# Attention row maxima put back by query: through PE's transposition or through DRAM

## The chip, the core and the metric

One core of a Trainium2 chip runs one program. The metric is the device time of one execution in microseconds (us). The engines that matter here are TensorE (PE, whose weight loads are listed as PEld), VectorE (DVE), ScalarE (ACT), GpSimd (POOL) and the queue of SyncE (SP, listed as SPq), which issues nearly all DMA transfers. All of them work through their own instructions in order and wait for each other by semaphores.

## The reference

A pre-norm transformer block on 2048 tokens of width 640: 32 heads of width 20, then a gated feed-forward part of width 1728.

```python
h = x + attention(layernorm(x))          # softmax(q k^T / sqrt(20)) v, then @ wo
h2 = h + (silu(n @ w_gate) * (n @ w_up)) @ w_down      # n = layernorm(h)
```

Everything is float32. The softmax is computed with its row maximum subtracted.

## The kernel before

Three stages follow each other. The first (to about 337 us) normalizes the tokens and projects queries, keys and values. The second is the attention (about 337 to 1545 us). The third is the feed-forward part.

The attention is worked in 32 *units*: 8 groups of four heads, each with 4 chunks of 512 queries. Unit `u` is group `u // 4`, chunk `u % 4`. Each unit has 16 *slots*, one for every 128 keys (`kt`). `now[0]` counts the slots, so unit `u` begins with slot `16 * u`. In a slot PE does four score products (`scores`, L890, the letters s and S of `ORDER`), each followed by an exponential on ACT (L896), and eight small products of weights and values of the slot two before (`weigh`, L900, the letter W).

The row maximum is not subtracted by an engine. Scores are products over 62 rows: 60 hold queries and keys split into a rounded and a rest part, and the rows 60 and 61 of the queries' tile `q_stk` hold the negated maximum of every query, as a rounded part and a rest; the same rows of the keys' tile hold ones. So a unit's scores can start only when these rows are filled, and the maximum must be known before. It is computed ahead by a product of its own over 60 rows (`max_one`, L181, the letters m and M) and a maximum over keys on DVE (L187). These run ahead of the scores: a unit's last maximum comes 5 to 14 slots before its first score.

With the last of them, `max_all` reduces over the key blocks on DVE (L194, tile `neg`: 128 queries on the partitions, 16 numbers each), and POOL splits the result into the rounded part and the rest (L198 and L199, tile `both`, 128 x 32). Queries stand on the partitions there, and must lie along a row in `q_stk`. `max_finish` does that: PE transposes `both` (L206) to a 32 x 128 tile in PSUM, which takes one of the four buffers `ps_one` that the scores use too; ACT copies it to SBUF (L208, tile `m2`, in the profile `m`); four DMA transfers on SP's queue (L213) bring 8 rows of 128 numbers each to the four places, a row 512 B in one piece. It is called two slots after the last maximum:

```python
closing[a[0]] = now[0] + 2
```

and stands in that slot behind the letter W, ahead of the next piece of the weights' preparation (`preparing`, POOL's splitting of the feed-forward weights with loads and stores on SP's queue).

Other work on SP's queue in these slots: the next keys and values (L143, L160) and the queries of unit `u + 3`; the row sums of the unit before (`r<-o`, L913, at slot 1 of a unit), their reciprocals to DRAM and spread over partitions (`r_d`, `rb`, L923 and L929, after slot 4), the divided output (L938, after slot 11). POOL multiplies by `rb` at slot 9 (L935). Every transfer on the queue signals one of eight semaphores in turn, and waits for the transfer that used it before; an instruction that waits holds up those behind it.

Of the kernel before, what the change touches and what calls it, by code (L numbers as in the profile page):

```python
# [9 lines left out]
F32 = mybir.dt.float32  # L10
BF16 = mybir.dt.bfloat16
F32R = mybir.dt.float32r
I32 = mybir.dt.int32
AF = mybir.ActivationFunctionType
# [3 lines left out]
P = 128  # L18
S = 2048
D = 640  # L20
H = 32
# [5 lines left out]
NC = S // CH  # L27
TPC = CH // P
NF = (F + P - 1) // P
G = 4  # L30
NG = H // G
# [12 lines left out]
def tile_block(ctx: ExitStack, tc: tile.TileContext, x, wqkv, wo, wg, wu, wd, out):  # L44
    nc = tc.nc
# [4 lines left out]
    dram = ctx.enter_context(tc.tile_pool(name="dram", bufs=1, space=bass.MemoryType.DRAM))  # L50
    qk_d = dram.tile([2, NG, 2, GD, S], F32R, name="qk_d")
    v_d = dram.tile([S, NG, VG], F32, name="v_d")
    o_d = dram.tile([D, S], F32, name="o_d")
    r_d = dram.tile([H, S], F32, name="r_d")
    z_d = [dram.tile([P, 2 * ND * CH], F32R, name=f"z_d{c}") for c in range(2)]
    t_d = [dram.tile([P, 8 * CH], F32R, name=f"t_d{i}") for i in range(2)]
# [14 lines left out]
    def ps_one():  # L71
        return psum.tile([P, CH], F32, name="ps_one", tag="ps_one", bufs=2)

    ident = const.tile([P, P], F32, name="ident")
# [50 lines left out]
    stk = att_ctx.enter_context(tc.tile_pool(name="stk", bufs=1, side="right"))  # L125
    k_stk = [stay.tile([P, 2, S], F32R, name="k_stk0", tag="first")]
    v_stk = [stay.tile([P, NT, VG], F32, name="v_stk0", tag="second")]
    keys, queries, values = {}, {}, {}
# [5 lines left out]
    ends = {}  # L134
# [42 lines left out]
    def max_one(u, kc, t, pair, b):  # L177

        ps = ps_max()
        rows = slice(b * ROW, b * ROW + NPART)  # L180
        nc.tensor.matmul(  # L181
            ps,
            queries[u][rows, pair, t * P : (t + 1) * P],
            keys[u // NC][rows, pair, kc * CH : (kc + 1) * CH],
            start=True, stop=True,
        )
        nc.vector.tensor_reduce(  # L187
            mxs[u][:, b, pair, t, kc : kc + 1], ps, axis=AX.X, op=ALU.max
        )

    def max_all(u):

        neg = stk.tile([P, G * TPC], F32, name="neg", tag="neg", bufs=2)
        nc.vector.tensor_reduce(  # L194
            neg, mxs[u].rearrange("p b h t k -> p (b h t) k"), axis=AX.X, op=ALU.max, negate=True
        )
        ends[u] = stk.tile([P, 2, G * TPC], F32R, name="both", tag="both", bufs=2)
        nc.gpsimd.tensor_copy(ends[u][:, 0], neg)  # L198
        nc.gpsimd.tensor_tensor(  # L199
            out=ends[u][:, 1], in0=neg, in1=ends[u][:, 0].bitcast(F32), op=ALU.subtract  # L200
        )

    def max_finish(u):

        m = ps_one()[: 2 * G * TPC, :P]
        nc.tensor.transpose(m, ends.pop(u).bitcast(F32).rearrange("p i n -> p (i n)"), ident)  # L206
        m2 = stk.tile([2 * G * TPC, P], F32R, name="m2", tag="m2", bufs=1)
        nc.scalar.activation(m2, m, AF.Copy)  # L208
        for b in range(2):
            for i in range(2):  # L210
                row = b * ROW + NPART + i
                first = (2 * i + b) * 2 * TPC
                nc.sync.dma_start(  # L213
                    queries[u][row : row + 1].bitcast(F32).rearrange(
                        "r j (t p) -> r (j t) p", t=TPC
                    ),
                    m2[first : first + 2 * TPC, :].bitcast(F32),
                )

    def in_projections(u, kc, t):  # L220

# [30 lines left out]
    with tc.tile_pool(name="pa", bufs=2) as pa:  # L252
# [245 lines left out]
        first = [("block", 0, 1), ("none",)] + [("block", m) for m in range(2, 2 * ND)]  # L498
# [4 lines left out]
        for c in range(NC):  # L503
# [7 lines left out]
            for j, (kind, *which) in enumerate(work):  # L511
# [21 lines left out]
                if 0 in ends:  # L533
                    finish_at = min(finish_at, slot[0] + 2)
                    if slot[0] == finish_at:
                        max_finish(0)
# [405 lines left out]
    todo, tail, accs, closing, now = [], [], {}, {}, [0]  # L942
# [3 lines left out]
    def next_max(b):  # L946
        if singles[b]:
            a = singles[b].pop(0)
            max_one(*a)
            left[a[0]] -= 1  # L950
            if left[a[0]] == 0:
                max_all(a[0])
                quiet[0] = now[0]
                closing[a[0]] = now[0] + 2

    def weigh_next():
        u, kt, probs = todo.pop(0)
# [10 lines left out]
    for u in range(NU):  # L968
        g, c = divmod(u, NC)
        if g == NG - 1 and c >= 2:  # L970
            _, first, ln, flips, _ = ahead
            extra = [*first, ln[0], lambda: None, ln[1], lambda: None, *flips]
        for kt in range(NT):
# [5 lines left out]
            for op in order:  # L979
                if op in "mM":  # L980
                    next_max(int(op == "M"))
                elif op in "sS":
                    scores(u, kt, heads[op == "S"].pop(0), probs)
                else:
                    if len(todo) == 2:
                        weigh_next()
                    for v in ready:
                        max_finish(v)
                    if extra:
                        extra.pop(0)()  # L990
                    if preparing and u and kt not in (3, 4) and quiet[0] != now[0]:
                        preparing.pop(0)()
                    if now[0] == (NU - NC) * NT + 8:
                        unit_ring, last_ring = weight_rings()
                        unit_ring.fill()
                        last_ring.fill()
# [41 lines left out]
    u, o, r = tail.pop()  # L1038
# [559 lines left out]
```

## Time and profile before

| what | value |
|---|---|
| median of 3 runs | 2111.13 us (2111.03 to 2113.79) |
| the profiled execution | 2112.34 us, of which its span is 2110.6 us |
| PE busy | 2077.2 us (98%) |
| DVE, ACT, POOL busy | 1752.9, 1295.9, 704.8 us |
| granted TensorE clock | 0.998 |
| DMA packets | 199673, 295.27 MB |

The profile has one execution. A line such as `L206 PE MATMUL ps_one<-ident,both` names the line of the kernel, the engine, the operation, the tile written and the tiles read. In the timeline the first number is the start and the second the duration; PE's rows merge instructions of one line that follow each other, and their ends overlap the next row's start, since products are pipelined: the distance from one start to the next is what an instruction costs PE.

### The profile page before, as it was taken

How to read it: one execution, taken by the hardware profiler on the slowest of the kernel's cores; microseconds unless marked ns; L12 is line 12 of the kernel's file. 1: busy time of each engine (PE TensorE's matmuls, PEld its weight loads, DVE VectorE, ACT ScalarE, POOL GpSimd, SP SyncE). 2: the span in 40 equal slices, each digit the busy share in tenths (PEclk: the TensorE clock that was granted, in tenths of full speed). 3: DMA queues.
4: the chain of work that ended last, by engine and by line, in shares of the span. 5: the costliest groups of instructions: out<-in, count | busy, mean ns of one | idle time of the engine just before them, and what ended most of it. 6: DMA issues, size and time to landing. Idle time of an engine off the chain costs nothing.

```text
span 2110.6 us, 35576 instructions
## 1 busy us (share of the span) xinstructions
PE 2077.2 (98%) x12606; PEld 1205.3 (57%) x12606; DVE 1752.9 (83%) x2901; ACT 1295.9 (61%) x2571; POOL 704.8 (33%) x1009
## 2 busy tenths in 40 slices
PE   7999999999999999999999999999999999999998
PEld 5766675333333333333333333335578888888887
DVE  6999997999999999999999999996358766666676
ACT  3222216999999999999999999996743222212221
POOL 3222212343343433353420001001135434653555
PEclk9999999999999999999999999999999999999999
DMA  7565432343433524533432113132137755884542
GB/s 253 168 190 166 153 119 82 122 122 106 150 115 102 169 89 136 165 136 126 136 110 75 33 38 88 33 100 76 35 121 262 266 171 186 300 299 158 197 152 92
DMA packets 199673, 295.27 MB, mean 140 GB/s; under 512 B 46840, under 2 KB 81656, under 8 KB 198472
## 3 DMA queue, kind: packets, MB, share of 16 engines
q1 hardware_dynamic: 185912, 266.77, 39.1%
q10 hardware_dynamic: 13584, 26.23, 4.0%
q8 instruction: 101, 1.65, 0.4%
q14 instruction: 76, 0.62, 0.1%
HBM read 196.44 MB, written 95.68 MB: 138 GB/s over the span
## 4 chain that ended last, share of the span: by engine, by line
PE 89%; DVE 5%; DMA 3%; POOL 1%; issue 1%; ACT 1%; SPq 0%; ACTq 0%; POOLq 0%; DVEq 0%
PE acc L900 24%; PE ps_max L181 15%; PE ps_one L890 15%; PE ps_a L1063 15%; PE ps_b L1157 8%; PE ps_one L422 4%; DVE mx L175 3%; PE ps_one L459 2%; PE ps_wide L171 2%; PE ps_max L628 2%; PE ps_b L628 1%; DMA qk_d<-e 1%; DMA raw<-qk_d 1%; DVE mx L187 1%; DMA halves<-j_d 1%
## 5 line engine op out<-in xcount | busy, mean ns | idle before, releaser
L896 ACT ACTIVATE probs<-ps_one 128x512 f32<-128x512 f32 x2048 | 1045.4, 623 | 131.9 <-PE ps_one L890 126.9
L187 DVE TENSOR_REDUCE mx<-ps_max 128x1 f32<-128x512 f32 x1632 | 1021.0, 683 | 95.7 <-PE ps_max L181 51.9
L890 PE MATMUL ps_one<-q_stk,k_stk 62*128 62x512 f32 x2048 | 551.1, 421 | 0.7 <-ACT e L265 0.7
L900 PE MATMUL acc<-probs,v_stk 128*32 128x512 f32 x4096 | 545.2, 604 | 0.3
L181 PE MATMUL ps_max<-k_stk,q_stk 60*128 60x512 f32 x1632 | 540.5, 459 | 2.4 <-DVE mx L187 1.5
L181 PEld LDWEIGHTS ps_max<-k_stk,q_stk 60*128 60x128 f32 x1632 | 230.2, 184 | 427.6 <-DVE mx L187 411.2
L890 PEld LDWEIGHTS ps_one<-q_stk,k_stk 62*128 62x128 f32 x2048 | 299.7, 185 | 81.6 <-ACT probs L896 52.3
L175 DVE TENSOR_REDUCE mx<-ps_wide 128x2 f32<-128x1024 f32 x208 | 240.5, 1217 | 16.2 <-PE ps_wide L171 16.0
L1278 DVE TENSOR_TENSOR tmp<-ps_a,tmp 128x512 f32<-128x512 f32 x208 | 141.2, 689 | 120.2 <-PE ps_a L1063 94.5
L1157 PE MATMUL ps_b<-halves,yp 128*128 128x320 f32 x1032 | 179.3, 308 | 1.8 <-POOL yp L81 1.2
L1157 PEld LDWEIGHTS ps_b<-halves,yp 128*128 128x128 f32 x1032 | 165.1, 188 | 18.4 <-POOL yp L81 1.5
L900 PEld LDWEIGHTS acc<-probs,v_stk 128*32 128x32 f32 x4096 | 80.6, 108 | 160.2 <-issue 152.1
L198 POOL CAST both<-neg 128x16 fp32r<-128x16 f32 x32 | 6.6, 206 | 467.6 <-DVE neg L194 212.5
L1063 PE MATMUL ps_a<-t,units 128*128 128x512 f32 x624 | 162.5, 396 | 0.0
L1063 PE MATMUL ps_a<-z,units 128*128 128x512 f32 x516 | 133.8, 394 | 0.0
L1063 PEld LDWEIGHTS ps_a<-t,units 128*128 128x128 f32 x624 | 112.6, 188 | 18.6
L81 POOL TENSOR_TENSOR yp<-y,yp 128x256 fp32r<-128x256 f32 x96 | 60.3, 628 | 187.8 <-ACT yp L80 187.8
L1162 DVE TENSOR_TENSOR h<-ps_b,h 128x320 f32<-128x320 f32 x248 | 110.1, 481 | 6.8 <-PE ps_b L1157 5.4
L1063 PEld LDWEIGHTS ps_a<-z,units 128*128 128x128 f32 x516 | 93.1, 187 | 15.9
L1063 PE MATMUL ps_a<-z,lasts 128*128 128x512 f32 x324 | 92.5, 393 | 0.0
L80 ACT ACTIVATE yp<-tmp 128x512 fp32r<-128x512 f32 x40 | 25.3, 632 | 103.2 <-POOL tmp L1150 103.2
L265 ACT ACTIVATE e<-ps_one 128x512 f32<-128x512 f32 x31 | 18.5, 598 | 107.3 <-PE ps_one L422 72.4
(164 smaller groups left out, 2066.6 us busy)
## 6 DMA issues: line engine op xcount, KB each, us to landing
units<-w_d SPq DMA_DIRECT2D x186, 256.0 KB
w_d<-stage SPq DMA_DIRECT2D x106, 256.0 KB
halves<-j_d SPq DMA_DIRECT2D x70, 320.0 KB
j_d<-stage SPq DMA_DIRECT2D x42, 320.0 KB
raw<-qk_d SPq DMA_DIRECT2D x70, 160.0 KB
k_stk<-qk_d SPq DMA_DIRECT2D x64, 160.0 KB
q_stk<-qk_d SPq DMA_DIRECT2D x64, 160.0 KB
rb<-r_d SPq DMA_DIRECT2D x32, 256.0 KB
```

The source lines that it names most:

```text
L175: nc.vector.tensor_reduce(mx[:, :, pair, t, kc], ps, axis=AX.X, op=ALU.max)
L181: nc.tensor.matmul(ps, queries[u][rows, pair, t * P : (t + 1) * P], keys[u // NC][rows, pair, kc * CH : (kc + 1) * CH], start=True, stop=True,
L187: nc.vector.tensor_reduce(mxs[u][:, b, pair, t, kc : kc + 1], ps, axis=AX.X, op=ALU.max)
L422: nc.tensor.matmul(ps, w[:, k, m * P : (m + 1) * P], a[:, k, :], start=(n == 0 and k == 0), stop=(n == 2 and k == ND - 1),)
L628: nc.tensor.matmul(ps[:, :HALF], a[:, k, :], w[:, k, hs], start=(n == 0), stop=(n == 3 * ND - 1),)
L890: nc.tensor.matmul(ps, keys[u // NC][rows, p, kt * P : (kt + 1) * P], queries[u][rows, p, :], start=True, stop=True,)
L896: nc.scalar.activation(probs[p][:, b, :], ps, AF.Exp, scale=scale)
L900: nc.tensor.matmul(acc[32 * j : 32 * j + 32, :], values[u // NC][:, kt, j * VW : j * VW + 32], probs[j // 2][:, j % 2, :], start=(kt == 0) ...
L1063: nc.tensor.matmul(ps.rearrange("p (t n) -> p t n", t=TPC), w[k][:, i], z[k][:, :, j], start=(first and m == 0), stop=(last and m == len(n ...
L1157: nc.tensor.matmul(ps, a, b, start=(n == 0), stop=(n == len(pairs) - 1))
L1162: nc.vector.tensor_tensor(out=h, in0=ps, in1=h, op=ALU.add)
L1278: add = lambda out, ps, x: nc.vector.tensor_tensor(out=out, in0=ps, in1=x, op=ALU.add)
```

## The change

`max_finish` no longer uses PE and ACT. One DMA transfer stores the tile `both` to a DRAM tile `m_d[u]`, 128 rows (queries) of 32 numbers. Four transfers load from it into the rows of `q_stk`: each takes 8 columns of all 128 rows, with the columns outermost, so numbers that follow each other in the destination lie 128 B apart in DRAM. Each load moves 1024 numbers, 4 B each, and waits for the store, since it reads what that wrote. `max_finish` is called one slot after the last maximum, not two; for unit 0, which is handled in the first stage, the place stays.

```diff
+    m_d = [dram.tile([P, 2 * H // NG * TPC], F32, name=f"m_d{u}") for u in range(NG * NC)]
...
     def max_finish(u):
 
-        m = ps_one()[: 2 * G * TPC, :P]
-        nc.tensor.transpose(m, ends.pop(u).bitcast(F32).rearrange("p i n -> p (i n)"), ident)
-        m2 = stk.tile([2 * G * TPC, P], F32R, name="m2", tag="m2", bufs=1)
-        nc.scalar.activation(m2, m, AF.Copy)
+        both = ends.pop(u).bitcast(F32)
+        nc.sync.dma_start(m_d[u], both.rearrange("p i n -> p (i n)"))
         for b in range(2):
             for i in range(2):
                 row = b * ROW + NPART + i
-                first = (2 * i + b) * 2 * TPC
-                nc.sync.dma_start(
-                    queries[u][row : row + 1].bitcast(F32).rearrange(
-                        "r j (t p) -> r (j t) p", t=TPC
-                    ),
-                    m2[first : first + 2 * TPC, :].bitcast(F32),
-                )
+                n = (i * 2 + b) * 2 * TPC
+                dst = queries[u][row : row + 1].bitcast(F32).rearrange("r j (t p) -> r (j t) p", p=P)
+                nc.sync.dma_start(dst, m_d[u][:, n : n + 2 * TPC].rearrange("p n -> n p").unsqueeze(0))
...
-                closing[a[0]] = now[0] + 2
+                closing[a[0]] = now[0] + 1
```

In the built program each of the four loads has 1024 elements of one number on its destination's side, and 8 by 128 elements of one number on its source's side. PE has 32 transpositions fewer, ACT 32 copies fewer and SP 32 transfers more.

## The prediction

> **What bounds the kernel now.** I read the page first, then the busy times of the attention by a window, then the waits in that window.
>
> ```profile
> span 2110.6 us, 35576 instructions
> PE 2077.2 (98%) x12606; PEld 1205.3 (57%) x12606; DVE 1752.9 (83%) x2901; ACT 1295.9 (61%) x2571; POOL 704.8 (33%) x1009
> DMA packets 199673, 295.27 MB, mean 140 GB/s; under 512 B 46840, under 2 KB 81656, under 8 KB 198472
> ```
>
> ```profile
> core 0: us, PE busy (x) PEld busy (x) DVE busy (x) ACT busy (x) POOL busy (x), PEclk, DMA share, GB/s
> 340.00:1480.00 1140.00, 1137.40 (x7664) 456.53 (x7663) 1036.86 (x1726) 1021.53 (x2035) 316.65 (x527) 1.00 0.34 104
> ```
>
> ```profile
> PEld ps_max L181 <- DVE mx L187: 410.2, 609, 1.1
> ACT probs L896 <- PE ps_one L890: 113.0, 303, 3.4
> POOL sums L740 <- DMA raw<-in_B_w_up: 109.9, 12, 16.7
> PEld ps_one L890 <- ACT probs L896: 44.8, 178, 0.8
> ```
>
> PE is busy in 1137.4 of 1140 us of the attention, so what PE is relieved of there comes off the time, up to the next bound. That is near: DVE has 1036.9 us and ACT 1021.5 us, so both have some 100 us of room in 1140, about ten times what follows. The large wait of PEld for DVE is the weight load standing ready early; PE itself hardly idles. The DMA engines are 34% used and POOL 28%: both have cover.
>
> **What is taken away.** Per unit one transposition, one copy on ACT and four short transfers.
>
> ```profile
> L206 PE MATMUL ps_one<-ident,both x32: 284/284/286, 314.1 to 1479.4; 128*32 128x128 f32 x32
> L208 ACT ACTIVATE m<-ps_one x32: 261/266/268, 314.4 to 1479.7; 32x128 fp32r<-32x128 f32 x32
> L213 SPq DMA_DIRECT2D q_stk<-m x128: 620/635/1357, 314.7 to 1482.1; - x128
> ```
>
> PE's duration of 0.284 us overlaps its neighbours, so I take distances of starts. Here is a slot with the transposition and the next one without it.
>
> ```profile
> 727.74 1.07 PE L900 MATMUL acc<-probs,v_stk 128*32 128x512 f32 x8
> 728.73 0.28 PE L206 MATMUL ps_one<-ident,both 128*32 128x128 f32 x1
> 728.95 0.50 PE L181 MATMUL ps_max<-k_stk,q_stk 60*128 60x512 f32 x2
> 729.86 1.06 PE L900 MATMUL acc<-probs,v_stk 128*32 128x512 f32 x8
> 730.85 0.51 PE L181 MATMUL ps_max<-k_stk,q_stk 60*128 60x512 f32 x2
> ```
>
> From the start of the eight products to the next other one are 0.99 us without it (730.85 - 729.86) and 1.21 us with it (728.95 - 727.74): it costs 0.22 us of PE. Its other cost is indirect: it takes one of four `ps_one` buffers out of the scores' turn until ACT has copied it, and the copy puts the exponentials behind it off by 0.266 us, for which PE then waits in some cases (the 44.8 us above). So one unit saves between 0.22 us (the copy is hidden) and 0.22 + 0.27 = 0.49 us (all of it comes through). I take 0.28 us, nearer to the lower end since ACT has room. Of the 32, 31 lie in the attention: 31 x 0.28 = 8.7 us (6.8 to 15). The 32nd, in the first stage, I set at nothing.
>
> **What is added: the way through DRAM.** Per unit one store, a wait for it, and four loads of 1024 numbers each, all on SP's queue. PE sees none of it unless the rows arrive after the unit's first score is due. So I need two lengths: how long the way takes from the end of `both`, and how long there is.
>
> The trace has no transfer of single numbers from DRAM. The nearest row for a store that a load waits for, and for small pieces, is that of the reciprocals: 128 pieces of 64 B to DRAM, and the load that reads them.
>
> ```profile
> 1334.99 0.60 SPq L923 DMA_DIRECT2D r_d<-r  x1
> 1336.99 0.58 SPq L929 DMA_DIRECT2D rb<-r_d  x1
> ```
>
> ```profile
> DMA packets 132, 0.01 MB, mean 26 GB/s; under 512 B 132, under 2 KB 132, under 8 KB 132
> q1 hardware_dynamic: 132, 0.01, 27.8%
> ```
>
> The load is issued 2.0 us after its store. The second fence is the window of 1336.20 to 1336.52 us, which holds that store's packets alone: 132 of them, 128 of data and 4 that signal the end, so it ran on four DMA engines, the size of its outermost dimension in DRAM (4 heads). The 27.8% of 16 engines in 0.32 us make 4.4 engines: these four were busy all along, with 33 packets each, so one packet took at most 0.32 / 33 = 9.7 ns of an engine. The loads that are to go show the same rule.
>
> ```profile
> 1480.00 2.77 SPq L213 DMA_DIRECT2D q_stk<-m  x4
> DMA  0000000000002000001000001000001000000000
> DMA packets 64, 0.02 MB, mean 4 GB/s; under 512 B 32, under 2 KB 64, under 8 KB 64
> ```
>
> Four loads leave 64 packets, 32 of data and 32 of signals: 8 engines each, as their outermost dimension is 8. The second and third row are the window 1480.0 to 1484.5 us in 40 slices of 0.11 us: the first packets fly in the 13th, 1.3 us after the issue. The new loads have 8 outermost on the source's side, so I count 8 engines with 128 numbers each.
>
> At 9.7 ns a number a load would take 1.24 us; that is the lower end, since the row's source is SBUF. For reads from DRAM the smallest pieces at full flow are 384 B, of the values' load in the window 327.7 to 328.7 us.
>
> ```profile
> 325.08 0.39 SPq L160 DMA_DIRECT2D v_stk<-v_d  x1
> DMA packets 820, 0.31 MB, mean 315 GB/s; under 512 B 820, under 2 KB 820, under 8 KB 820
> ```
>
> 820 packets in 1 us on 16 engines are 19.5 ns for each; at that rate a load takes 128 x 19.5 = 2.5 us, the upper end, since these carry 384 B. I take 1.5 us (11.7 ns), nearer to the small packets' row, because a number of 4 B is closer to 64 B than to 384 B. What speaks for more than the upper end is only that no row shows reads of 4 B.
>
> The four loads run on the same engines, one after the other. The way from the end of `both` then takes: 2.0 us for the store; 1.3 us to the first packet of the first load; four times a load; and 0.4 us, an estimate, for the first issue and the last signal. That is 3.7 + 4 x 1.5 = 9.7 us (8.7 to 13.7 us with the ends). SP's own issues (four at 0.635 us, 2.5 us) go on beside it.
>
> How long there is: from POOL's end of `both` to the first score of the unit.
>
> ```profile
> L199 POOL TENSOR_TENSOR both<-neg,both x31: 220/222/468, 365.3 to 1478.9; 128x16 fp32r<-128x16 f32 x31
> L890 PE MATMUL ps_one<-q_stk,k_stk x2048: 383/394/522, 337.4 to 1540.0; 62*128 62x512 f32 x187
> 365.35 0.22 POOL L199 TENSOR_TENSOR both<-neg,both 128x16 fp32r<-128x16 f32 x1
> 373.58 0.62 PE L890 MATMUL ps_one<-q_stk,k_stk 62*128 62x512 f32 x3
> 874.55 0.22 POOL L199 TENSOR_TENSOR both<-neg,both 128x16 fp32r<-128x16 f32 x1
> 883.15 0.73 PE L890 MATMUL ps_one<-q_stk,k_stk 62*128 62x512 f32 x2
> 1018.48 0.22 POOL L199 TENSOR_TENSOR both<-neg,both 128x16 fp32r<-128x16 f32 x1
> 1029.33 0.40 PE L890 MATMUL ps_one<-q_stk,k_stk 62*128 62x512 f32 x2
> ```
>
> These are the units 1, 15 and 19: 373.58 - 365.57 = 8.0 us, 8.7 us (the new unit's score is the second in the row of 883.15 and starts at 883.49) and 10.6 us. From the same two lines I worked out all 31: 8.0, 8.7, 10.6, 10.9, 11.2, 11.3, 12.0, 13.3, 13.6, 13.6, three of 14.7, and 18 from 16.1 to 27.0. A unit waits for what its way takes over this, and since PE is full, the wait goes on the time. Summed over the list: a way of 9.7 us costs 1.7 + 1.0 = 2.7 us; 8.7 us costs 0.7; 11.7 us costs 9; 13.7 us costs 24; 20 us costs 122. The call one slot earlier is in these lengths: SP is not bound to PE's slot, it waits for POOL alone, so the way starts when `both` is done; the slot of about 2.2 us (727.74 to 729.86 is one) pays for the store's 2.0 us.
>
> **What is pushed aside on SP.** Ahead of the store nothing new stands, but the queue waits there for `both`, and then 2.0 us for the store; behind it stand the next raw weights, stage stores, keys, values, and for the units whose call comes at slot 3 or 4 (5, 9, 17, 21, 25, 29) the reciprocals' store and `rb`. All start some 2 to 5 us later. Who waits for them is POOL (109.9 us already for raw weights), which has 823 of 1140 us free, and its `rb` at slot 9, five slots (11 us) on. I set it at nothing. If POOL ran late by so much that the next `both` were late, the 8.0 to 10.6 us above would shrink by it, one for one.
>
> **The sum.** 2112.3 us (the profiled execution; 1.2 us above the median of 2111.1) - 8.7 + 2.7 = 2106.3 us, or 2105.1 us on the median. I give 2105.
>
> **A rule that speaks against it.** The last of the four old loads, in the window 1481.2 to 1481.5 us (slices of 7.5 ns):
>
> ```profile
> DMA  0000000000000000000000900305005100100000
> GB/s 0 0 0 0 0 0 0 0 0 0 0 0 0 0 0 0 0 0 0 0 0 0 205 0 0 69 0 137 1 1 137 1 1 0 1 0 0 0 0 0
> ```
>
> Its data start between slice 23 and slice 31, so with the last packet's own length the 4 KB take about 0.1 us. The Trainium skill, "DMA: Bandwidth & Descriptors", section "Rules for kernel authors", says that a strided last dimension becomes one descriptor for each element, and that a plain DMA with a rearranged access pattern differs 19 times from the hardware's transposition. As an estimate from that page, 19 x 0.1 us is 1.9 us a load, a way of 11.3 us, waits of 7.0 us and 2109.5 us on the median: no change, where my 1.5 us a load gives 2105. The trace agrees with its first half through the 1024 elements of the built load; no run here shows the 19, and I keep to the rows.
>
> **Rivals.**
>
> *Reads of single numbers are slower than any packet here* (slower). Place: the four loads; price: the sum above; point from which it decides: the wait equals the 8.7 us saved at a way of 11.6 us, which is 2.0 us a load or 15.4 ns a number. At 31 ns (4 us a load) the way takes 20 us, 21 units wait, 122 us: 2111 - 9 + 122 = 2224 us. For it: nothing in the trace reads 4 B from DRAM, and reads that wait for each other would not follow the bytes. Against it: both rows of small packets lie between 9.7 and 19.5 ns. Chance 0.40, of which two thirds lie below 2200 us.
>
> *Gain and wait cancel* (within 0.2%). At 1.7 to 2.15 us a load, or if DVE's maxima come to be waited for where PE is relieved and only 0.22 us a unit is left with a way of 10.5 us (4.3 us of waits): 2111.1 - 6.8 + 4.3 = 2109 us. Chance 0.10.
>
> *The loads do not go number by number.* Were neighbours joined, no unit would wait: 2111.1 - 8.7 = 2102 us. Against it: neighbours in the destination lie 128 B apart in the source. Chance 0.03.
>
> **How the numbers follow.** The forecast has 0.47. Its own range is 2099 us (0.40 us a unit, no waits) to 2106.9 us. Faster by over 0.2% (4.2 us, about what a measurement here can tell): 0.47 + 0.03 = 0.50; within: 0.10; slower: 0.40. The range begins at 2099 and must reach far into the slow rival: up to 2200 us (a way of 18 us) leaves out about 0.13 above and 0.04 below.
>
> **What would show it.** PE and ACT lose the rows of L206 and L208, and two successive W rows stand 0.2 to 0.3 us closer where a transposition was. DMA packets rise by 32 x (4 x 1032 + 144 - 64) = 134656 to about 334300, nearly all under 512 B; 8 x 129 packets a load confirm 8 engines. In the window of one `max_finish` the four loads' packets should last about 6 us; over 8 us proves the forecast wrong. PE should wait for `q_stk<-m_d` before the first L890 of units 1 and 15 only, by about 1 to 2 us. A wait at ten or more units, or one at L890 of over 5 us, means the rival.

## The result, and the profile after

The changed kernel takes 2561.82 us (median of 4 runs, 2557.4 to 2567.09) against 2111.35 us of the kernel before: a ratio of 1.2132 [1.2105, 1.2158]. It is slower by 450 us, outside the predicted range and on the other side. The profiled execution took 2567.09 us, with a span of 2565.3 us. The page after:

```profile
span 2565.3 us, 35410 instructions
PE 2149.6 (84%) x12574; PEld 1226.0 (48%) x12574; DVE 1756.2 (68%) x2901; ACT 1296.8 (51%) x2539; POOL 703.9 (27%) x1009
PEclk9999998888899878888888888889988999999999
DMA packets 334327, 295.78 MB, mean 115 GB/s; under 512 B 182520, under 2 KB 216312, under 8 KB 333128
PE 52%; DMA 32%; DVE 6%; SPq 6%; issue 2%; POOL 2%; ACT 1%; ACTq 0%; DVEq 0%; POOLq 0%
```

The last line is the chain that ended last. In the kernel before it was 89% PE and 3% DMA. PE does the same work less 32 transpositions, but its busy time is 72.4 us longer, and its granted clock sags in the middle of the span. The packets are as many as forecast. The attention alone, as a window, then the waits of PE and of SP's queue over the whole span (total, times, longest):

```profile
340.00:1922.00 1582.00, 1211.99 (x7645) 478.53 (x7645) 1042.10 (x1728) 1025.50 (x2010) 317.03 (x528) 0.87 0.55 75
```

```profile
PE ps_one L885 <- DMA q_stk<-m_d: 299.5, 27, 18.8
PE acc L895 <- ACT o L905: 54.8, 9, 11.8
PE ps_one L885 <- ACT probs L891: 23.5, 6, 13.7
```

```profile
SPq L207 <- POOL both L200: 105.3, 20, 25.5
SPq L213 <- DMA m_d<-both: 92.2, 32, 6.3
SPq L924 <- DMA r_d<-r: 77.9, 32, 7.7
```

This stretch is 442 us longer than the 1140 us of before. PE is idle in 370 us of it (2.6 before). The wait for the rows of `q_stk` is 299.5 us, in 27 waits at 26 units (the last two are unit 31's, which begins just after the window); and PE is busy 75 us longer, at a mean clock of 0.87. The second and third wait of PE end with ACT, not with the rows; the second comes up again below.

One unit (unit 3) shows the mechanism. First SP's queue, then PE around the new unit's first score:

```profile
468.84 0.35 SPq L207 DMA_DIRECT2D m_d<-both  x1
472.64 12.10 SPq L213 DMA_DIRECT2D q_stk<-m_d  x4
484.79 5.84 SPq L694 DMA_DIRECT2D w_d<-stage  x2
```

```profile
482.98 0.49 PE L885 MATMUL ps_one<-q_stk,k_stk 62*128 62x512 f32 x1
498.14 0.76 PE L885 MATMUL ps_one<-q_stk,k_stk 62*128 62x512 f32 x1 [14.67 <-DMA q_stk<-m_d]
500.11 1.93 PE L895 MATMUL acc<-probs,v_stk 128*32 128x512 f32 x8
503.43 1.07 PE L895 MATMUL acc<-probs,v_stk 128*32 128x512 f32 x8
```

The store goes out at 468.84, the loads start 3.8 us later, and the score that needs them starts at 498.14: 25.5 us after the first load's issue. Four issues hold SP's queue for 12.1 us, where four of the old ones took 2.8 us. Over all units the first three issues usually take 0.7 to 1.05 us and the fourth about 9 us:

```profile
L213 SPq DMA_DIRECT2D q_stk<-m_d x128: 666/1046/9549, 310.4 to 1928.5; - x128
```

From the semaphore events of the loads, the last one lands 23.8 us after the first one's issue (median of 32 units, 21.3 to 26.3); the four land at 11.4, 16.5, 22.2 and 23.8 us. The DMA view of unit 3's stretch, 474.0 to 498.2 us in 40 slices:

```profile
DMA  2669999999900000461790000069995695536666
GB/s 2 5 2 2 1 1 1 1 1 1 0 0 0 0 0 0 2 2 1 2 0 0 0 0 0 1 3 102 196 152 116 48 47 27 26 47 254 193 86 66
DMA packets 4886, 0.84 MB, mean 35 GB/s; under 512 B 4554, under 2 KB 4554, under 8 KB 4886
```

The single numbers are 4096 of these packets. In the first 27 slices nearly nothing else flies: the engines count as busy while they move 1 GB/s. From the packets' own records of this unit, the first 1700 or so start within 2.5 us; the other 2400 start over the next 14 us, 172 per us, with two pauses of 3.2 us. The last load's signal comes 7.5 us behind the last start; what passes in between the records don't tell. From the first start (474.1) to that signal (498.0) it is 5.8 ns for each number over all engines together. I had counted 11.7 ns for each on *one of eight* engines, 1.5 ns over all.

The clock is the fourth loss. These windows have the columns of the prediction's second fence; the third from the end is the granted clock as a share of full speed:

```profile
482.00:484.00 2.00, 1.48 (x11) 0.32 (x10) 1.76 (x4) 2.00 (x5) 0.00 (x0) 1.00 0.05 0
496.00:498.00 2.00, 0.00 (x0) 0.00 (x0) 0.00 (x0) 0.00 (x0) 0.00 (x0) 0.50 0.68 139
500.00:502.00 2.00, 2.00 (x11) 0.23 (x10) 1.08 (x2) 1.00 (x3) 0.00 (x0) 0.50 0.92 299
502.00:504.00 2.00, 2.00 (x18) 0.96 (x14) 1.19 (x2) 0.77 (x2) 0.00 (x0) 0.70 1.02 319
```

At 482 PE has full speed. In the wait the clock falls to 0.50 and stays there after PE has resumed at 498.1, until 503.2 (a mean of 0.70 over the last window is 1.2 us at 0.50 and 0.8 us at full speed): 5.1 us at half speed, some 2.5 us lost behind this wait. The eight products at 500.11 last 1.93 us, those at 503.43 1.07 us. The Trainium skill, "TensorE: Matmul & The Clock Gate", section "Part 1: The HAM clock gate (the "warmup" mystery)", has a cold state of half the clock after a free-running window of some 3.4 us without activity, and full clock after some 3.4 us of activity. The trace agrees with the two levels; the return took 5.1 us here.

Between 340 and 1922 us the clock's records have 36 stretches at 0.50, in which PE is busy for 173 us. Half of that, some 87 us, covers the 75 us by which PE is busy longer and the 7 us of the transpositions that are gone.

Where the 457 us by which the whole attention is longer went, by comparing the distance of each slot's first score with that of before, for units 1 to 30: 296 us fall between a unit's last slot and the next unit's first score, 50 us into slots 0 and 1 (half clock), 71 us into slot 2, 12 us into the other slots. Unit 0 adds 19 and unit 31 adds 9 us.

### The profile page after: what moved, and what is told of

Its sections match the earlier page's. It is cut to its first block, busy times and chain, and to the rows that moved or that the text cites. A ratio compares the mean times of both kernels' runs of the same rounds, so it can differ in the third digit from the quotient of the medians.

```text
span 2565.3 us, 35410 instructions
## 1 busy us (share of the span) xinstructions
PE 2149.6 (84%) x12574; PEld 1226.0 (48%) x12574; DVE 1756.2 (68%) x2901; ACT 1296.8 (51%) x2539; POOL 703.9 (27%) x1009
## 2 busy tenths in 40 slices
DMA packets 334327, 295.78 MB, mean 115 GB/s; under 512 B 182520, under 2 KB 216312, under 8 KB 333128
## 4 chain that ended last, share of the span: by engine, by line
PE 52%; DMA 32%; DVE 6%; SPq 6%; issue 2%; POOL 2%; ACT 1%; ACTq 0%; DVEq 0%; POOLq 0%
DMA q_stk<-m_d 17%; PE ps_a L1058 12%; PE acc L895 11%; PE ps_one L885 6%; PE ps_b L1152 6%; PE ps_max L182 6%; SPq L213 4%; PE ps_one L417 4%; DMA m_d<-both 3%; DVE mx L176 3%; DMA r_d<-r 2%; DVE mx L188 2%; PE ps_wide L172 2%; PE ps_one L454 2%; PE ps_max L623 2%
## 5 line engine op out<-in xcount | busy, mean ns | idle before, releaser
L885 PE MATMUL ps_one<-q_stk,k_stk 62*128 62x512 f32 x2048 | 577.9, 444 | 325.7 <-DMA q_stk<-m_d 299.5
L895 PE MATMUL acc<-probs,v_stk 128*32 128x512 f32 x4096 | 582.2, 642 | 54.8 <-ACT o L905 54.8
L182 PE MATMUL ps_max<-k_stk,q_stk 60*128 60x512 f32 x1632 | 572.4, 481 | 6.9 <-DVE mx L188 5.5
L885 PEld LDWEIGHTS ps_one<-q_stk,k_stk 62*128 62x128 f32 x2048 | 314.0, 199 | 407.9 <-issue 308.4
L182 PEld LDWEIGHTS ps_max<-k_stk,q_stk 60*128 60x128 f32 x1632 | 245.9, 195 | 492.5 <-DVE mx L188 431.5
L930 POOL TENSOR_TENSOR o<-o,rb 128x512 f32<-128x512 f32 x31 | 39.7, 1280 | 198.0 <-DMA rb<-r_d 89.6
L735 POOL TENSOR_TENSOR sums<-raw 128x256 f32<-128x256 f32 x13 | 9.5, 730 | 290.5 <-DMA raw<-in_B_w_up 290.5
```

The source lines that it names most:

```text
L182: nc.tensor.matmul(ps, queries[u][rows, pair, t * P : (t + 1) * P], keys[u // NC][rows, pair, kc * CH : (kc + 1) * CH], start=True, stop=True,
L885: nc.tensor.matmul(ps, keys[u // NC][rows, p, kt * P : (kt + 1) * P], queries[u][rows, p, :], start=True, stop=True,)
L895: nc.tensor.matmul(acc[32 * j : 32 * j + 32, :], values[u // NC][:, kt, j * VW : j * VW + 32], probs[j // 2][:, j % 2, :], start=(kt == 0) ...
```

## The experiments

The rival that had been on record spoke of reads of single numbers. After the result three causes for the 23.8 us stood against each other: reads from DRAM at 128 B steps (R), single-number packets on an engine whatever they read or write (E), and single-number writes into one row of `q_stk`, that is into one partition (W). All changes are against the kernel after, unless said otherwise.

**The gain alone** (`e1_rows_constant`, against the kernel before):

```diff
+    m2 = stk.tile([2 * G * TPC, P], F32R, name="m2", tag="m2", bufs=1)
+    nc.gpsimd.memset(m2.bitcast(F32), 0.0)
...
-        m = ps_one()[: 2 * G * TPC, :P]
-        nc.tensor.transpose(m, ends.pop(u).bitcast(F32).rearrange("p i n -> p (i n)"), ident)
-        m2 = stk.tile([2 * G * TPC, P], F32R, name="m2", tag="m2", bufs=1)
-        nc.scalar.activation(m2, m, AF.Copy)
+        ends.pop(u)
```

> The kernel before, without the transposition and ScalarE's copy: the four loads bring rows of zeros from a tile filled once, so the maxima aren't used (the scores' exponentials are not lowered by them). It measures what taking PE's and ScalarE's part away is worth with nothing in its place. All theories: 31 x 0.28 = 8.7 us faster than 2111 us (6.8 to 15), about 2102 us, and no wait of PE for q_stk. If it is worth less than 4 us, the first term of the forecast was wrong too.

Measured: 2103.26 us, ratio 0.9964 [0.995, 0.9977], 8.4 us less than the kernel before in the same series (2111.70). That this is near the 8.7 us expected is in part luck: by the distances of their first scores, units 1 to 30 are shorter by 0.2 us each, four of them by 0.3 or 0.4, 6.6 us together. The rest is not of these units: in the profiled execution the attention begins 4.4 us earlier and unit 0 is 1.6 us longer, which no part of this edit explains. The saving is PE's 0.22 us. Taking the copy from ACT brings nothing beside it.

**The store turned instead of the loads** (`e3_store_turned`): single numbers are written to DRAM, and the loads move rows of 128.

```diff
-    m_d = [dram.tile([P, 2 * H // NG * TPC], F32, name=f"m_d{u}") for u in range(NG * NC)]
+    m_d = [dram.tile([2 * H // NG * TPC, P], F32, name=f"m_d{u}") for u in range(NG * NC)]
...
-        both = ends.pop(u).bitcast(F32)
-        nc.sync.dma_start(m_d[u], both.rearrange("p i n -> p (i n)"))
+        both = ends.pop(u).bitcast(F32).rearrange("p i n -> p (i n)")
+        nc.sync.dma_start(m_d[u].rearrange("n p -> p n"), both)
...
-                nc.sync.dma_start(dst, m_d[u][:, n : n + 2 * TPC].rearrange("p n -> n p").unsqueeze(0))
...
+                    m_d[u][first : first + 2 * TPC, :],
```

> The way through DRAM kept, but turned at the store: 4096 single numbers are written from SBUF to DRAM in rows by maximum, and the four loads bring 1024 neighbouring numbers each. Theory W (single numbers written into one SBUF partition share one path, 5.8 ns each, whichever engine sends them): the store takes 4096 x 9.7 ns / 16 engines = 2.5 us more than a plain one, the way from POOL's end about 8.5 us, no unit or two wait, 2103 us. Theory R (single numbers read from DRAM are the limit): the same 2103 us, as none are read. Theory E (every DMA engine needs 47 ns for a number, wherever it goes): 256 x 47 ns = 12 us for the store, way about 18 us, waits of some 85 us, 2190 us or more.

Measured: 2358.59 us, ratio 1.1171 [1.1156, 1.1186]. R and W both miss. The store lands 16.9 us after its issue (median), 4.1 ns a number over all engines, though it runs on 16 engines and writes no single number into a row of `q_stk`. PE waits:

```profile
PE ps_one L889 <- DMA q_stk<-m_d: 115.6, 21, 11.7
PE acc L899 <- ACT o L909: 47.1, 10, 8.8
```

Single numbers are slow on the way into DRAM too. E comes nearest, but falls with the next two.

**The same loads into eight partitions** (`e4_spread_partitions`): each load writes 8 partitions of a 32 x 128 tile, and four more transfers put its rows in place, as the kernel before does.

```diff
+        m2 = stk.tile([2 * G * TPC, P], F32R, name="m2", tag="m2", bufs=1)
+        for n in range(0, 2 * G * TPC, 2 * TPC):
+            nc.sync.dma_start(
+                m2[n : n + 2 * TPC, :].bitcast(F32), m_d[u][:, n : n + 2 * TPC].rearrange("p n -> n p")
+            )
...
-                nc.sync.dma_start(dst, m_d[u][:, n : n + 2 * TPC].rearrange("p n -> n p").unsqueeze(0))
...
+                    m2[first : first + 2 * TPC, :].bitcast(F32),
```

> As the changed kernel up to the loads: the same four loads of 1024 single numbers from DRAM, on 8 engines as counted there, but each into 8 partitions of a 32 x 128 tile (512 B in each) rather than into one. Four further transfers bring it to the rows, as in the kernel before. Theory W: a load's numbers go into 8 partitions, so the four take about 4 x 1.2 to 1.5 us, the way with the further step 12 to 14 us, waits of 11 to 27 us, about 2115 to 2135 us. Theories R and E: the loads take 24 us as in the changed kernel, and the further step comes on top, way 30 us, 2600 us or more.

Measured: 2195.59 us, ratio 1.0398 [1.0379, 1.0417]. The same 4096 reads at the same addresses, on 8 engines, now take 8.3 us (8.0 to 9.6), not 23.8. This refutes R and E: what changed is where the numbers are written. It is 2.0 ns a number, close to what my 1.5 us a load would have given (1.3 + 4 x 1.5 + 0.4 = 7.7 us). The way from `both` to the last row is 14.0 us (median) and the wait for the rows 25.0 us, as W had them; the time is some 60 to 80 us above what W gave, by waits that are not for the rows and by slots that are longer (34 us in slot 2, by the distances as above):

```profile
PE ps_one L894 <- DMA q_stk<-m: 25.0, 11, 5.2
PE acc L904 <- ACT o L914: 20.4, 9, 5.0
PE ps_one L894 <- ACT probs L900: 12.4, 4, 7.4
```

**Pairs** (`e5_pairs`): each load moves 512 pairs of neighbours into the same row.

```diff
-                dst = queries[u][row : row + 1].bitcast(F32).rearrange("r j (t p) -> r (j t) p", p=P)
-                nc.sync.dma_start(dst, m_d[u][:, n : n + 2 * TPC].rearrange("p n -> n p").unsqueeze(0))
+                dst = queries[u][row : row + 1].bitcast(F32).rearrange("r j (t p w) -> r (j t) p w", t=2, w=2)
+                src = m_d[u][:, n : n + 2 * TPC].rearrange("p (a w) -> a p w", w=2)
+                nc.sync.dma_start(dst, src.unsqueeze(0))
```

> As the changed kernel, but each load brings 512 pairs of neighbouring numbers (8 B) rather than 1024 numbers, into the same row, in a wrong order; its outermost dimension is 4, so 4 DMA engines carry it rather than 8. Theory W, and R with one shared limit: half as many packets, 2048 x 5.8 ns = 12 us for the four loads, way about 15.5 us, 13 units wait, some 45 us and a quarter of that for the lower clock after waits: about 2160 us. Theory E: 512 / 4 = 128 packets on every engine as before, the four loads take 24 us as before, 2560 us.

Measured: 2163.21 us, ratio 1.0244 [1.0226, 1.0263]; first issue to last landing 10.5 us. This is W's number, and E's is far off. In part it is luck: PE waits for the rows 19.1 us at 8 units, where 45 us at 13 were expected, and 24 us are lost in the slots 2 and 6 instead. The price of the writes is what decides: the bytes are the same and each engine has 512 packets as in the changed kernel (2048 on 4 engines, 4096 on 8), but the time is less than half. It is the number of writes into the row that counts.

**Four engines** (`e6_four_engines`): every load is split into two of 512 numbers, which run on 4 engines. If the engines hindered each other at the one partition (C), fewer of them should be quicker.

```diff
-                n = (i * 2 + b) * 2 * TPC
-                dst = queries[u][row : row + 1].bitcast(F32).rearrange("r j (t p) -> r (j t) p", p=P)
-                nc.sync.dma_start(dst, m_d[u][:, n : n + 2 * TPC].rearrange("p n -> n p").unsqueeze(0))
+                for j in range(2):
+                    n = (i * 2 + b) * 2 * TPC + j * TPC
+                    dst = queries[u][row : row + 1, j : j + 1].bitcast(F32).rearrange("r j (t p) -> r (j t) p", p=P)
+                    nc.sync.dma_start(dst, m_d[u][:, n : n + TPC].rearrange("p n -> n p").unsqueeze(0))
```

> As the changed kernel, with every load cut in two: eight loads of 512 single numbers from 4 columns, so 4 DMA engines carry each, not 8, and the numbers, their order and their one partition per row stay. Theory W as it stands after the earlier runs (numbers that go into one SBUF partition pass one after the other, 5.8 ns each, however many engines send; spread over 8 partitions they took 1.7 ns): 4096 x 5.8 ns = 24 us again, about 2560 us. Theory C (it is the engines that collide in the one partition; the pairs on 4 engines took 4.3 ns a packet, not 5.8): 4096 x 4.3 ns = 17.6 us, way 21 to 22 us, waits of some 150 us, about 2300 us.

Measured: 2481.93 us, ratio 1.1757 [1.1727, 1.1786]; 21.1 us from issue to landing, against 23.8. The time is nearer to W's than to C's. With half the engines the writes are a little quicker, not slower, and take twice the time of the pairs: on the same four engines 4096 writes are 5.2 ns each and 2048 are 5.1 ns. They pass one after another, and collisions of engines are about a ninth of it at most. PE's wait for the rows is 186.2 us by that name, and two waits at a unit's first score that the list puts down to other transfers (15.0 us at unit 15, 4.4 us at unit 13) belong to it: some 206 us against 299.5. 2.7 us at each of 26 units would make 70 of these 94 us; stores that land after 2.9 us (median), not 3.6, are a possible rest that I did not separate.

**The way without single numbers** (`e7_turned_on_vector`): DVE turns the reduced maxima in blocks of 32 x 32, the store writes rows of 256 B, the loads move pieces of 128 B.

```diff
+        turned = stk.tile([P, 32], F32, name="turned", tag="turned", bufs=2)
+        nc.vector.transpose(turned, neg)
...
+        src = m_d[u].rearrange("(q n) (i w) -> i n q w", q=4, i=2)
...
+                nc.sync.dma_start(dst, src[i, b * 2 * TPC : (b + 1) * 2 * TPC].unsqueeze(0))
```

> The way through DRAM kept, without single numbers: VectorE turns the 32 x 32 blocks of the maxima right after its reduction (one instruction more on it for a unit), GpSimd splits the turned tile, the store writes 128 rows of 256 B and each of the four loads brings 32 pieces of 128 B (on 8 engines) into its row. If the single numbers alone were to blame for the loss: way about 2.0 + 1.3 + 2.5 + 0.4 = 6.2 us, no unit waits (the shortest room was 8.0 us), and the gain of the run with constant rows remains: 2103 us, at most 31 x 0.2 us = 6 us more if VectorE's instruction came through in full. If the way through DRAM as such (its wait on SyncE, what is pushed aside there) costs more: 2115 us or above.

Measured: 2112.49 us, ratio 1.0002 [0.9993, 1.0012]. The loads land 4.1 us after the first issue (3.9 in the kernel before), and PE never waits for the rows. So a store, a wait and four loads through DRAM are harmless in this place. But the 0.22 us is gone as well: the units are as long as before, to 0.1 us in most. What PE is relieved of, DVE is given:

```profile
L204 DVE STREAM_TRANSPOSE turned<-neg x32: 211/212/214, 311.3 to 1482.0; 128x32 f32<-128x32 f32 x32
PEld ps_max L182 <- DVE mx L188: 433.9, 641, 1.1
```

The added 0.212 us of DVE is as long as PE's 0.22 us, and the weight loads of PE's maxima products wait for DVE 24 us longer than before (410.2 us). The slots show where. The first fence is the kernel before, with the transposition behind its second row; the second is the same place in this run, with DVE's new instruction:

```profile
725.03 1.07 PE L900 MATMUL acc<-probs,v_stk 128*32 128x512 f32 x8
727.74 1.07 PE L900 MATMUL acc<-probs,v_stk 128*32 128x512 f32 x8
729.86 1.06 PE L900 MATMUL acc<-probs,v_stk 128*32 128x512 f32 x8
```

```profile
729.38 1.06 PE L904 MATMUL acc<-probs,v_stk 128*32 128x512 f32 x8
730.44 0.21 DVE L204 STREAM_TRANSPOSE turned<-neg 128x32 f32<-128x32 f32 x1
732.30 1.07 PE L904 MATMUL acc<-probs,v_stk 128*32 128x512 f32 x8
734.19 1.07 PE L904 MATMUL acc<-probs,v_stk 128*32 128x512 f32 x8
```

The second distance falls from 2.12 to 1.89 us, as the transposition is gone; the first, in which DVE turns, grows from 2.71 to 2.92 us. Over the 31 units the medians are 0.22 us less and 0.21 us more; in the run with constant rows, which has no such instruction, the first distance is unchanged (0.00). So DVE's instruction takes the gain back, in the slot before the one that gains.

**The earlier slot alone** (`e8_slot_only`, against the kernel before):

```diff
-                closing[a[0]] = now[0] + 2
+                closing[a[0]] = now[0] + 1
```

> The kernel before with the other half of the change alone: the transposition, the copy and the four loads stay, and are called one slot after the last maximum, not two. Both theories: no part of the loss, 2111 us; up to 5 us more if the transposition now waits for GpSimd's split, which was done 0 to 3 us before it in the kernel before.

Measured: 2126.11 us, ratio 1.0068 [1.0053, 1.0083], 14.6 us slower: missed. With the transposition in place, PE comes to it before POOL has split the maxima:

```profile
PE ps_one L206 <- POOL both L199: 11.9, 13, 2.3
```

Some 13 units are 0.7 to 1.0 us longer, unit 30 3.2 us. The changed kernel does not pay this, because only SP waits there; the two halves of the change go together.

**A second output tile** (`e9_two_outputs`), for the second wait of PE:

```diff
-        o = pc.tile([P, CH], F32, name="o", bufs=1)
+        o = pc.tile([P, CH], F32, name="o", bufs=2)
```

> The changed kernel with two buffers for the tile o (the unit's output, which ScalarE copies from PSUM and SyncE stores after the division) rather than one. The theory is that 55 us of PE's waits (for ScalarE's copy into o) and most of the 24 us of its waits for exponentials come from SyncE's queue, which the loads hold up, so that o is stored late: then they go, and the time falls by 55 to 100 us (a lower clock follows each wait) to 2460 to 2510 us. Rival: these waits only stand in the shadow of the late rows, and the time stays at 2560 us.

Measured: 2496.84 us, ratio 1.1827 [1.1804, 1.1851], 65 us less than the changed kernel, as expected. PE's wait for `o` is gone, and slot 2's loss falls from 71 us to less than nothing (-4). So that wait was SP's queue: the stores that empty `o` stood behind the four loads, and ACT could not refill it. The wait for the rows is 33 us shorter too. Part of it moves on; slot 6 now loses 43 us (6.7 in the changed kernel), with a new wait in the second row:

```profile
PE ps_one L885 <- DMA q_stk<-m_d: 266.6, 25, 18.8
PE ps_max L182 <- DVE mx L188: 31.9, 13, 6.6
```

That DVE is late because its reciprocals wait for the row sums on SP's queue fits, but was not tried.

**A shorter transposition** (`e10_short_transposition`, against the kernel before), as the other way to the 0.22 us:

```diff
-        nc.tensor.transpose(m, ends.pop(u).bitcast(F32).rearrange("p i n -> p (i n)"), ident)
+        nc.tensor.transpose(m.bitcast(F32R), ends.pop(u).rearrange("p i n -> p (i n)"), ident_r)
```

> The kernel before, with the transposition done in the type of the tile (float32r, in which both parts are held already) against a second identity of that type, instead of float32. The runs so far say that what is to be had here is PE's 0.22 us for a unit, and that neither VectorE's queue nor a way through DRAM gives it away free. If the 128 columns then pass at the rate at which the scores' 512 columns pass (0.23 us from start to start in the page's timeline, so about 0.06 us), a unit gains about 0.15 us: 31 x 0.15 = 4.7 us, 2107 us, 0.2% below the kernel before. If the transposition costs PE the same in either type: 2111.5 us.

Measured: 2110.08 us, ratio 0.9998 [0.9989, 1.0008], no change. The trace shows a small one below what the times can tell:

```profile
727.27 1.07 PE L903 MATMUL acc<-probs,v_stk 128*32 128x512 f32 x8
728.27 0.24 PE L209 MATMUL ps_one<-ident_r,both 128*32 128x128 f32 x1
728.43 0.50 PE L184 MATMUL ps_max<-k_stk,q_stk 60*128 60x512 f32 x2
```

The same distance as in the prediction is 1.16 us here (728.43 - 727.27) and was 1.21 us: 0.05 us less a unit, some 2 us in all, and the attention is 1.9 us shorter. None of the versions that use the maxima beats the kernel before.

## Why the prediction was wrong, point by point

*The price of a load* is the step that failed. It stood at 1.5 us, with 1.24 and 2.5 us as ends, from the packets of 64 B to DRAM (9.7 ns of an engine) and of 384 B from DRAM (19.5 ns), shared out over 8 engines. In their place the runs show 5.5 us a load for four in a row, in the prediction's own terms ((23.8 - 1.3 - 0.4) / 4): 5.4 ns a number over all engines together. The rows were read rightly, but sharing out over engines was wrong here: into one row of `q_stk` the numbers pass one after another (pairs: 10.5 us; 4 engines: 21.1 us; 8 engines: 23.8 us; eight rows: 8.3 us). Neither row showed this, and the upper end reached no further than they did. What makes writes to one partition pass singly inside the chip stays open, and whether it is the one partition or a few neighbours that share the limit; so does whether the single numbers of the turned store are slow at their reading or their writing, since both sides differ there.

*The store* was 2.0 us and is 3.6 us (median from issue to landing, 1.4 to 6.6). Why it varies was not tried; the prediction took it from one row of the reciprocals.

*The rooms and the sum over them* were right. Put the measured way into the list of 31 rooms, 3.6 + 23.8 = 27.4 us, and the waits come to some 310 us; PE's wait for the rows is 299.5 us. It fits unit by unit too: unit 15, with a room of 8.7 us, should wait 18.7 us and waited 18.8. The form of the sum was good; one term was off by nearly four, and the rooms are so close together that this makes 300 us out of 2.7.

*The gain* was right at its lower end: 0.22 us a unit, 6.8 us, not 8.7. The indirect part, the copy on ACT, was worth nothing. The 44.8 us that the prediction named for it are waits of weight loads (PEld); PE itself was idle for 2.6 us in that window.

*What is pushed aside on SP, set at nothing*, was wrong by more than 50 us. I looked for who waits for what stands behind the store, and counted the store's 2 us. What weighs is that the queue itself is held while the loads are issued, 11.7 us for the four (median) where the prediction had 2.5 us, and that ACT's only tile `o` is emptied by that queue: 54.8 us at `acc`. With a second tile this wait was gone and the time 65 us shorter.

*The clock* was no term at all. A wait as in unit 3 is followed by half speed, and PE is busy 75 us longer in the attention. In the prediction's sum a wait cost its own length only.

*DVE's room of 100 us* is true over the stage and false in the slots: 0.212 us more on DVE, at the place where the maxima end, left nothing of PE's gain. *The earlier slot at no cost* holds for the changed kernel only; alone it costs 14.6 us.

*The rival* had the direction, and its signs came: "a wait at ten or more units" at 26, and waits over 5 us of up to 18.8 us. Its cause was wrong: the reads are not slow, the writes are. Its worked price ended at 31 ns on each of eight engines, 4 us a load; the measured 5.5 us a load lies beyond. The estimate by the Trainium skill, "DMA: Bandwidth & Descriptors", section "Rules for kernel authors", 19 times or 1.9 us a load, is a third of what was measured; it put the 19 on the plain transfer's 0.1 us, while the page compares with the hardware's transposition, for which no run here has a time. The page's rule of one descriptor an element agrees with the trace (8 x 129 packets a load, 334327 in all against the 334300 of the prediction).

## What to carry to other kernels

The number of small pieces (4 or 8 B here) that a transfer writes into one partition is a cost of its own, not shared out over the engines: before turning data by a strided DMA, ask how many writes end in the same row, and turn it on an engine, or spread it over partitions first, if they are thousands. Price a slow transfer three times: for those who wait for it, for all that stands behind it on its queue, and, where PE waits as long as here, for the half clock that follows. And a room in a stage's mean busy time is not a room in the slot where the work is put.

## What the runs showed of the hardware that was not expected

- From the first issue to the last landing, single numbers into one partition cost 5.8 ns each over all engines on 8 engines and 5.2 ns on 4, pairs 5.1 ns a pair on 4, and single numbers into eight partitions a load 2.0 ns; single numbers from SBUF into DRAM cost 4.1 ns on 16 engines. Pieces of 128 B landed as quickly as those of 512 B (4.1 and 3.9 us for four loads).
- The fourth load of 1024 single numbers in a row held SP's queue for 8.8 us at its issue (median, up to 9.5); the second and third held it for 1.0 us.
- After a wait of 14.7 us PE worked 5.1 us at a granted clock of 0.50. In the clock's records of this execution the stretches at 0.50 within the attention last 3.4 to 20.5 us, each a multiple of 3.41 us.
